# A router's logits on Trainium2: gate weights as the streamed operand, tokens as the stationary one

## The chip, the cores and the metric

The kernel runs on one core of a Trainium2 chip. The core has five engines that run side by side and wait for each other through semaphores: TensorE (PE; its weight loads are listed apart, as PEld), VectorE (DVE), ScalarE (ACT), GpSimd (POOL) and SyncE (SP), which issues most DMAs. Times are device microseconds (us) of one execution; the number that counts is the median of the runs.

## The reference, cut to what matters

Attention with a memory term over 4 batches, 8 heads and 576 positions gives x, 2304 tokens of 512 features. A mixture of 8 experts follows. Its router computes logits, takes the exponential, and normalises rows and columns eight times:

```
def _moe_ref(x, w_gate, w1, w2):
    N, D = x.shape                      # 2304, 512
    E = w_gate.shape[1]                 # 8
    logits = x @ w_gate
    logits = logits - logits.max()
    P = np.exp(logits)
    for _ in range(8):
        P /= P.sum(1, keepdims=True) + 1e-09
        P /= P.sum(0, keepdims=True) + 1e-09
        P *= N / E
    out = np.zeros((N, D), dtype=np.float32)
    for e in range(E):
        h = np.maximum(x @ w1[e], 0.0)
        ye = h @ w2[e]
        out += P[:, e:e + 1] * ye
```

## The kernel before, in words

Attention goes through 16 pairs of heads, one after another, in steps that overlap; the order of all instructions in it is written by hand: each step has a due time (pair number plus the number in the table WHEN), the steps are sorted by it, and every engine executes its own in that order. Each pair leaves 128 features of 576 tokens in two tiles, xh (rounded to a short mantissa) and xl (what the rounding dropped); `xh`, `xl` hold [128 features, 4 blocks of features, 2304 tokens].

The router's logits are made in five chunks of 512 tokens (the last has 256), `CHUNKS`. Three of them (0, 1, 2) stand in the hand-written order of attention, 0.33 of a pair after pairs 8, 12 and 16; two (3, 4) are tasks that are called between the parts of the first expert's product, outside the hand-written order.

`setup_router` (L173) puts the gate's weights into `wgp`, [128 features, 4 blocks, 128 columns]: columns 0 to 7 hold the rounded weights, 8 to 15 what the rounding dropped, and the other 112 are zeroed by a memset. `logits_a` (L707) uses one block of wgp, 128 by 128, as the stationary operand and streams 512 tokens of xh or xl past it: 8 matmuls for a chunk. The result has gate columns on partitions, so ScalarE copies 16 rows of it to `ls`. `logits_b` (L728) turns ls with small TensorE transposes, one for 128 tokens, into a second PSUM tile with tokens on partitions, and VectorE adds the two halves of 8 columns into `P`, [128 tokens, 18 blocks, 8 experts].

PSUM tiles of this kind come from a ring of six banks (`ps_s`, also called `ps_t`): each new tile takes the next bank, and waits until its last reader is done.

Other lines that are spoken of: L299, VectorE's subtractions that make ql and kl from the transposed q and k; L408, the scores; L540, transposes of the fifth block of exponentials; L648, the product with v; L678, GpSimd's subtraction that makes xl; L836 and L857, the first expert's two products.

Of the kernel before, what the change touches and what calls it, by code (L numbers as in the profile page):

```python
# [8 lines left out]
F32 = mybir.dt.float32  # L9
# [8 lines left out]
def kernel(  # L18
# [13 lines left out]
    nc = tc.nc  # L32
    B, H, S, D = q.shape
    NT, DM = out.shape
    E, _, F = w1.shape
    HP = H // 2
    KD = DM // 128
# [3 lines left out]
    CHUNKS = [(c, min(512, NT - c)) for c in range(0, NT, 512)]  # L41
# [8 lines left out]
    wst_p = ctx.enter_context(tc.tile_pool(name="wst", bufs=2))  # L50
    ps = ctx.enter_context(tc.tile_pool(name="ps", bufs=1, space=PSUM))

    xh = static.tile([128, KD, NT], F32R, name="xh")
    xl = static.tile([128, KD, NT], F32R, name="xl")
# [18 lines left out]
    ident = const.tile([128, 128], F32, name="ident")  # L73
    ones = const.tile([128, 128], F32, name="ones")
    wgp = const.tile([128, KD, 128], F32R, name="wgp")
# [21 lines left out]
    ps_t = ps_s  # L97
# [3 lines left out]
    def wst(w=512):  # L101
        wturn[0] += 1
        return wst_p.tile([128, w], F32, tag=f"wst{wturn[0] % 2}", name="wst", bufs=1)

    def f32(ap):
        return ap.bitcast(F32)
# [64 lines left out]
        nc.vector.tensor_copy(out=ogb, in_=g2[:, 1].unsqueeze(3).to_broadcast([128, HP, 2, 64]))  # L171

    def setup_router():  # L173
        nc.vector.memset(f32(wgp), 0.0)
        wgr = wst()
        wgv = wgr[:, 0:KD * E].rearrange("p (k e) -> p k e", e=E)
        nc.sync.dma_start(out=wgv, in_=wg.rearrange("(k p) e -> p k e", p=128))
        nc.vector.tensor_copy(out=wgp[:, :, 0:E], in_=wgv)
        nc.vector.tensor_tensor(
            out=wgp[:, :, E:2 * E], in0=wgv, in1=f32(wgp[:, :, 0:E]), op=ALU.subtract  # L180
        )
# [20 lines left out]
    }  # L202
    LATER = {
# [13 lines left out]
    def attention():  # L217
        with ExitStack() as actx:
# [66 lines left out]
            def steps(p):  # L285
# [398 lines left out]
            seq = [  # L684
                (p + WHEN[name] + LATER.get((p, name), 0.0), f)
                for p in range(NPAIR) for name, f in steps(p)
            ]
            for j in range(4):
                seq += [(0.5 + 0.5 * j + WHEN["w" + a], f) for a, f in zip("dhl", w_task(j))]
            for c, parts in enumerate(early_parts()):  # L690
                for i, t0, (a, d) in ((0, 8.33, "gA"), (1, 8.75, "gD")):
                    fs = (logits_a, logits_b)[i](c)
                    seq += [(4 * c + t0 + dt, f) for dt, f in zip((0.0, WHEN[a + d]), fs)]
                for j, fs in enumerate(parts):
                    t0 = 4 * c + 5 + j // 2 + (0.33, 0.75)[j % 2]
                    kinds = ("", "rA", "rD") if j < 2 else ("", "yD", "yS")
                    seq += [(t0 + WHEN.get(a, 0.0), f) for a, f in zip(kinds, fs)]
            seq += [(WHEN["sl"], load_gates), (WHEN["sg"], setup_gates)]
            seq.append((1.0, setup_router))
            seq.sort(key=lambda x: x[0])  # L700
            with tc.manual_schedule():
# [4 lines left out]
    lsd = {}  # L706

    def logits_a(c):
        c0, n = CHUNKS[c]

        def mm():
            lsd[c] = lp = ps_t()
            for a, x in enumerate((xh, xl)):
                for kt in range(KD):
                    nc.tensor.matmul(
                        out=lp[:, 0:n], lhsT=wgp[:, kt], rhs=x[:, kt, c0:c0 + n],
                        start=(a == 0 and kt == 0), stop=(a == 1 and kt == KD - 1),
                    )

        def take():  # L720
            lp = lsd[c]
            lsd[c] = ls = wst_p.tile([128, 512], F32, tag="ls", name="ls", bufs=1)[0:2 * E]
            nc.scalar.copy(out=ls[:, 0:n], in_=lp[0:2 * E, 0:n])

        return [mm, take]

    def logits_b(c):
        c0, n = CHUNKS[c]  # L728
        nt = n // 128

        def tr():
            ls = lsd[c]
            lsd[c] = lt = ps_t()
            for j in range(nt):
                nc.tensor.transpose(
                    lt[:, 16 * j:16 * j + 16], ls[:, 128 * j:128 * j + 128],
                    ident[0:2 * E, 0:2 * E],
                )

        def take():  # L740
            lv = lsd.pop(c)[:, 0:16 * nt].rearrange("p (t e) -> p t e", e=2 * E)
            pv_ = P[:, c0 // 128:c0 // 128 + nt]
            nc.vector.tensor_copy(out=pv_, in_=lv[:, :, 0:E])
            nc.vector.tensor_tensor(out=pv_, in0=lv[:, :, E:2 * E], in1=pv_, op=ALU.add)

        return [tr, take]

    def router_tasks():
        def both(f, c):
            for g in f(c):  # L750
                g()

        tasks = [lambda c=c, f=f: both(f, c) for c in (3, 4) for f in (logits_a, logits_b)]

        def max_a():
            nc.vector.reduce_max(mx[:, 0:1], P.rearrange("p t e -> p (t e)"), axis=AX.X)

        bank = {}

        def max_t():  # L760
            bank[0] = mt = ps.tile([128, 512], F32, tag="x", name="mt", bufs=1)
            nc.tensor.transpose(mt[:, 0:128], mx[:, 0:1].to_broadcast([128, 128]), ident)

        def max_b():
            mt = bank.pop(0)
            nc.vector.reduce_max(mx[:, 1:2], mt[:, 0:128], axis=AX.X)
            nc.vector.tensor_scalar_mul(mx[:, 1:2], mx[:, 1:2], -1.0)
            nc.scalar.activation(out=P, in_=P, func=AF.Exp, bias=mx[:, 1:2])

        def rows():  # L770
            nc.vector.reduce_sum(rs, P, axis=AX.X)
            nc.vector.tensor_scalar_add(rs, rs, 1e-9)
            nc.vector.reciprocal(out=rs, in_=rs)
            nc.vector.tensor_tensor(
                out=Pt, in0=P, in1=rs.unsqueeze(2).to_broadcast([128, NTILE, E]), op=ALU.mult
            )

        def colmat():
            bank[0] = cp = ps.tile([128, 512], F32, tag="x", name="cp", bufs=1)
            nc.tensor.matmul(  # L780
                out=cp[:, 0:NTILE * E], lhsT=ones, rhs=Pt.rearrange("p t e -> p (t e)"),
                start=True, stop=True,
            )

        def colsum():
            cp = bank.pop(0)
            nc.vector.reduce_sum(
                cs, cp[:, 0:NTILE * E].rearrange("p (t e) -> p e t", e=E), axis=AX.X
            )
            nc.vector.tensor_scalar_add(cs, cs, 1e-9)  # L790
            nc.vector.reciprocal(out=cs, in_=cs)
            nc.vector.scalar_tensor_tensor(
                out=P, in0=Pt, scalar=float(NT) / E,
                in1=cs.unsqueeze(1).to_broadcast([128, NTILE, E]), op0=ALU.mult, op1=ALU.mult,
            )

        tasks += [max_a, max_t, max_b]
        for _ in range(8):
            tasks += [lambda: None, rows, lambda: None, colmat, colsum][1:]

        def turn_p():
            bank[0] = mt = ps.tile([128, 512], F32, tag="x", name="mt", bufs=1)
            pf = wst()
            nc.vector.tensor_copy(
                out=pf[:, 0:144].rearrange("p (e t) -> p e t", e=E), in_=P.rearrange("p t e -> p e t")
            )
            nc.tensor.transpose(mt[0:126, 0:128], pf[:, 0:126], ident)
            nc.tensor.transpose(mt[0:18, 128:256], pf[:, 126:144], ident)

        def keep_p():  # L810
            mt, w = bank.pop(0), wst()
            rows_ = pd.rearrange("e (t c) -> (e t) c", c=128)
            nc.scalar.copy(out=w[0:126, 0:128], in_=mt[0:126, 0:128])
            nc.scalar.copy(out=w[0:18, 128:256], in_=mt[0:18, 128:256])
            nc.sync.dma_start(out=rows_[0:126], in_=w[0:126, 0:128])
            nc.sync.dma_start(out=rows_[126:144], in_=w[0:18, 128:256])

        return tasks + [turn_p, keep_p]
# [65 lines left out]
    def early_parts():  # L884
        def ps_f():
            return ps.tile([128, 512], F32, tag="f", name="f", bufs=1)

        return [first_parts(c, ps_f) for c in range(NEARLY)]
# [5 lines left out]
    def experts():  # L894
# [12 lines left out]
        ]  # L907
        acc = mg.tile([128, 2 * HT // 128, DM], F32, name="acc")
        tasks = router_tasks()
        tasks.reverse()  # L910

# [1050 lines left out]

    setup()
    attention()
    front.close()
    experts()
# [30 lines left out]
```

## Time and profile before

| what | us |
|---|---|
| runs shown | 1694.51, 1690.19, 1694.09 |
| median of them | 1694.09 |
| span of the profiled execution, first to last instruction | 1689.9 |
| TensorE busy in it | 1667.1 |
| VectorE, ScalarE, GpSimd busy | 1339.3, 692.2, 983.1 |
| attention, and the three early chunks of logits | 0 to about 244 |
| the two late chunks of logits | 247.7 to 257 |

The profile is of one execution; its own time is given only as the span. A row of the timeline has the start, the length, the engine, the line, the operation, the tiles (written<-read), stationary shape and streamed shape, and how many like it were merged; in square brackets stands how long the engine idled before it, and what ended that. A row of the chain has a start, a length and a line: it follows the work that ended last, back through what released each piece. A matmul's record is longer than the time until the next one may start, so its pace is read from starts.

### The profile page before, as it was taken

To read this page: it belongs to the slowest core of one execution; us is meant where nothing else is said; L and a number is where in the kernel's file an instruction comes from. 1 tells how busy PE (TensorE), PEld (TensorE's weight loads), DVE (VectorE), ACT (ScalarE), POOL (GpSimd) and SP (SyncE) were. 2 spreads that over 40 slices of the span, in tenths; PEclk is the share of its full clock that TensorE was granted. 3 is DMA by queue.
4 is the path that set the end of the run, shared out by engine and by line. 5 is a ranking of instruction groups with operands and counts; after the bars stand their busy time and mean duration, and the time that the engine had idled before them with its cause. 6 is when DMAs were issued, how large, how long until landed. Compare 5 with 4: busy or idle time off the path is not lost.

```text
span 1689.9 us, 29765 instructions
## 1 busy us (share of the span) xinstructions
PE 1667.1 (99%) x9779; PEld 1551.9 (92%) x9779; DVE 1339.3 (79%) x2805; ACT 692.2 (41%) x1724; POOL 983.1 (58%) x1036
## 2 busy tenths in 40 slices
PE   7999999999999999999999999999999999999998
PEld 6778778898998898889999999999999999999997
DVE  8877746867777777768898888989887878787887
ACT  7877752343433333334333333333243333333331
POOL 5755643578777877765556455455445544644561
PEclk9999999999999999999999999999999999999999
DMA  5443325478888888768787778677386767576663
GB/s 135 109 110 91 101 87 175 149 248 253 260 282 261 256 283 266 239 214 301 256 282 249 257 237 290 240 260 261 115 284 214 244 209 242 186 258 209 221 212 119
DMA packets 298145, 366.02 MB, mean 217 GB/s; under 512 B 80887, under 2 KB 176391, under 8 KB 297991
## 3 DMA queue, kind: packets, MB, share of 16 engines
q1 hardware_dynamic: 296215, 363.03, 66.8%
q8 instruction: 79, 1.29, 0.3%
q10 hardware_dynamic: 1776, 1.09, 0.2%
q14 instruction: 75, 0.61, 0.1%
HBM read 257.45 MB, written 106.58 MB: 215 GB/s over the span
## 4 chain that ended last, share of the span: by engine, by line
PE 91%; DVE 4%; DMA 2%; issue 1%; ACT 1%; POOL 0%; SPq 0%; DVEq 0%; ACTq 0%; POOLq 0%
PE s L1692 19%; PE s L1569 18%; PE s L857 14%; PE s L1111 10%; PE f L1569 6%; PE sx L1692 3%; PE f L1111 3%; PE x L648 2%; PE s L408 2%; PE f L1692 2%; PE s L1849 2%; PE s L489 1%; PE f L857 1%; PE f L836 1%; DVE temps L1548 1%; PE s L313 1%
## 5 line engine op out<-in xcount | busy, mean ns | idle before, releaser
L1548 DVE TENSOR_TENSOR temps<-s,temps 128x384 f32<-128x384 f32 x270 | 146.6, 553 | 91.6 <-PE s L1569 38.5
L1043 POOL TENSOR_TENSOR w1l<-raw,w1h 128x512 fp32r<-128x512 f32 x85 | 116.4, 1381 | 111.7 <-ACT w1h L1042 89.1
L1185 DVE SCALAR_TENSOR_TENSOR acc<-s,P,acc 128x512 f32<-128x512 f32 x168 | 123.1, 745 | 41.6 <-PE s L857 41.6
L857 PE MATMUL s<-w2h,hhh 128*128 128x512 f32 x372 | 146.0, 392 | 0.6 <-DVE acc L1185 0.6
L857 PE MATMUL s<-w2h,hhl 128*128 128x512 f32 x372 | 145.4, 391 | 0.0
L857 PE MATMUL s<-w2l,hhh 128*128 128x512 f32 x372 | 145.4, 391 | 0.0
L1548 DVE TENSOR_TENSOR m<-s,m 128x384 f32<-128x384 f32 x230 | 117.3, 550 | 7.5 <-PE s L1692 6.8
L1548 POOL TENSOR_TENSOR xl<-temps,xh 128x384 fp32r<-128x384 f32 x46 | 57.2, 1243 | 100.5 <-ACT xh L1590 100.5
L1590 ACT CAST xh<-temps 128x384 fp32r<-128x384 f32 x126 | 62.5, 513 | 118.1 <-DVE temps L1597 77.3
L1142 DVE TENSOR_TENSOR temps<-s,temps 128x384 f32<-128x384 f32 x132 | 71.4, 554 | 49.5 <-PE s L1111 39.4
L1569 PE MATMUL s<-xh,w1h 128*128 128x384 f32 x388 | 108.8, 335 | 0.0
L1597 DVE SCALAR_TENSOR_TENSOR temps<-temps,pb 128x384 f32<-128x384 f32 x180 | 105.5, 593 | 1.3
L1569 PE MATMUL s<-th,w1l 128*128 128x384 f32 x364 | 104.5, 334 | 0.0
L1569 PE MATMUL s<-th,w1h 128*128 128x384 f32 x356 | 102.3, 335 | 0.3 <-DVE temps L1548 0.3
L1076 POOL TENSOR_TENSOR w2l<-raw,w2h 128x512 fp32r<-128x512 f32 x62 | 97.5, 1591 | 2.8 <-ACT w2h L1075 2.8
L1095 ACT ACTIVATE hhh<-temps 128x384 fp32r<-128x384 f32 x100 | 52.5, 525 | 83.8 <-DVE temps L1142 82.8
L857 PEld LDWEIGHTS s<-w2h,hhh 128*128 128x128 f32 x372 | 69.9, 188 | 16.2 <-DVE acc L1185 2.6
L857 PEld LDWEIGHTS s<-w2h,hhl 128*128 128x128 f32 x372 | 69.8, 188 | 14.7
L857 PEld LDWEIGHTS s<-w2l,hhh 128*128 128x128 f32 x372 | 69.8, 188 | 13.7
L1096 DVE SCALAR_TENSOR_TENSOR hhl<-temps,hhh 128x384 fp32r<-128x384 f32 x100 | 81.3, 813 | 0.0
L1590 ACT CAST hb<-temps 128x384 fp32r<-128x384 f32 x90 | 46.1, 512 | 80.6 <-DVE temps L1597 79.9
L1548 POOL TENSOR_TENSOR temps<-temps,f 128x384 f32<-128x384 f32 x28 | 35.2, 1258 | 71.1 <-DVE hb L1548 40.8
(420 smaller groups left out, 5639.7 us busy)
## 6 DMA issues: line engine op xcount, KB each, us to landing
w1h<-cache SPq DMA_DIRECT2D x245, 256.0 KB
w1l<-cache SPq DMA_DIRECT2D x239, 256.0 KB
raw<-in_moe_w_dram SPq DMA_DIRECT2D x158, 256.0 KB
cache<-w1h SPq DMA_DIRECT2D x27, 896.0 KB
cache<-w1l SPq DMA_DIRECT2D x27, 896.0 KB
w2h<-cache SPq DMA_DIRECT2D x60, 256.0 KB
rawb<-in_moe_w_dram SPq DMA_DIRECT2D x32, 256.0 KB
cache<-w2h SPq DMA_DIRECT2D x31, 256.0 KB
```

What stands on the lines that cost most here:

```text
L857: nc.tensor.matmul(out=pt, lhsT=h_[:, f, cols], rhs=w[:, f], start=(n == 0), stop=(n == 5))
L1043: tt(out=wl[:, i:i + 2], in0=src, in1=f32(wh[:, i:i + 2]), op=ALU.subtract)
L1076: nc.gpsimd.tensor_tensor(out=wl[:, j], in0=raws[j], in1=f32(wh[:, j]), op=ALU.subtract)
L1096: late.append(lambda: nc.vector.scalar_tensor_tensor(out=hl[:, f, c], in0=src, scalar=0.0, in1=f32(hh[:, f, c]), op0=ALU.max, op1=ALU.subt ...
L1111: nc.tensor.matmul(out=pt[:, 0:HT], lhsT=w[:, wi, k], rhs=x[:, k], start=(n == 0), stop=(n == total - 1),)
L1142: nc.vector.tensor_tensor(out=o, in0=x, in1=y, op=ALU.add)
L1185: nc.vector.scalar_tensor_tensor(out=acc[:, j], in0=pt, scalar=P[:, t_, e:e + 1], in1=acc[:, j], op0=ALU.mult, op1=ALU.add,)
L1548: return lambda: eng.tensor_tensor(out=now_(o), in0=now_(x), in1=now_(y), op=op)
L1569: pe.matmul(out=bank[:, 0:HT], lhsT=w[:, a, k], rhs=x[b][:, k], start=bool(first and n == 0), stop=bool(last and n == 5),)
L1590: at(t, lambda: ac.copy(out=hop[j][n][0], in_=src), f"{n}H{j}")
L1597: at(t, lambda: dv.scalar_tensor_tensor(out=dst, in0=src, scalar=0.0, in1=pb[int(n[2]) - 1], op0=ALU.max, op1=ALU.mult), f"{n}F{j}")
L1692: pe.matmul(out=bank[n, a][:, 0:HT], lhsT=w[p][:, 128 * a:128 * a + 128], rhs=x[r], start=(j == js[0] and i == 0 and (n, a) not in held), ...
```

## The change

The operands of the logits change places. For each block of 128 tokens, xh and xl, 128 features by 128 tokens, are the stationary operand, and the 16 columns of wgp are streamed; four blocks of features times two (xh, xl) are eight matmuls for a block, 32 for a chunk of 512 tokens. The result has tokens on partitions at once. So ScalarE's copy to ls, the small transposes and the second PSUM tile are gone, as is the memset of the 112 columns, which nothing reads. `logits_b` is gone; its VectorE part, two instructions, is the second step of `logits_a` and takes its due time from "gD" after the matmuls, 0.42 of a pair earlier than before. For chunks 3 and 4 an empty task takes the place of logits_b.

```
     def setup_router():
-        nc.vector.memset(f32(wgp), 0.0)
...
             for c, parts in enumerate(early_parts()):
-                for i, t0, (a, d) in ((0, 8.33, "gA"), (1, 8.75, "gD")):
-                    fs = (logits_a, logits_b)[i](c)
-                    seq += [(4 * c + t0 + dt, f) for dt, f in zip((0.0, WHEN[a + d]), fs)]
+                seq += [(4 * c + 8.33 + dt, f) for dt, f in zip((0.0, WHEN["gD"]), logits_a(c))]
...
             lsd[c] = lp = ps_t()
-            for a, x in enumerate((xh, xl)):
+            for j in range(n // 128):
+                t = slice(c0 + 128 * j, c0 + 128 * j + 128)
                 for kt in range(KD):
-                    nc.tensor.matmul(
-                        out=lp[:, 0:n], lhsT=wgp[:, kt], rhs=x[:, kt, c0:c0 + n],
-                        start=(a == 0 and kt == 0), stop=(a == 1 and kt == KD - 1),
-                    )
+                    for a, x in enumerate((xh, xl)):
+                        nc.tensor.matmul(
+                            out=lp[:, 2 * E * j:2 * E * j + 2 * E], lhsT=x[:, kt, t],
+                            rhs=wgp[:, kt, 0:2 * E], start=(kt == 0 and a == 0),
+                            stop=(kt == KD - 1 and a == 1),
+                        )
 
         def take():
-            lp = lsd[c]
-            lsd[c] = ls = wst_p.tile([128, 512], F32, tag="ls", name="ls", bufs=1)[0:2 * E]
-            nc.scalar.copy(out=ls[:, 0:n], in_=lp[0:2 * E, 0:n])
-
-        return [mm, take]
-
-    def logits_b(c):
-        c0, n = CHUNKS[c]
-        nt = n // 128
-
-        def tr():
-            ls = lsd[c]
-            lsd[c] = lt = ps_t()
-            for j in range(nt):
-                nc.tensor.transpose(
-                    lt[:, 16 * j:16 * j + 16], ls[:, 128 * j:128 * j + 128],
-                    ident[0:2 * E, 0:2 * E],
-                )
-
-        def take():
-            lv = lsd.pop(c)[:, 0:16 * nt].rearrange("p (t e) -> p t e", e=2 * E)
+            nt = n // 128
+            lv = lsd.pop(c)[:, 0:2 * E * nt].rearrange("p (t e) -> p t e", e=2 * E)
             pv_ = P[:, c0 // 128:c0 // 128 + nt]
             nc.vector.tensor_copy(out=pv_, in_=lv[:, :, 0:E])
             nc.vector.tensor_tensor(out=pv_, in0=lv[:, :, E:2 * E], in1=pv_, op=ALU.add)
 
-        return [tr, take]
+        return [mm, take]
...
-        tasks = [lambda c=c, f=f: both(f, c) for c in (3, 4) for f in (logits_a, logits_b)]
+        tasks = [f for c in (3, 4) for f in (lambda c=c: both(logits_a, c), lambda: None)]
```

On TensorE, chunk 0 in the order of before, between the transposes of q and k for one pair and the product with v of the pair before it (x is the PSUM tile of that product, ls the copied logits):

```order
L330 MATMUL s<-ident,kraw_123 128x128
L331 MATMUL s<-ident,qraw_121 128x128
L715 MATMUL s<-xh,wgp 128x512 x4
L715 MATMUL s<-xl,wgp 128x512 x4
L648 MATMUL x<-eB,vs 64x320 x6
...
L489 MATMUL s<-ident,e 128x128 x11
L588 MATMUL s<-ident,qn_134 128x128
L735 MATMUL s<-ident,ls 128x16 x4
L540 MATMUL s<-ident,e_133 128x128 x4
```

The same place in the changed kernel, where the two rows of L714 alternate until there are 32 of them:

```order
L329 MATMUL s<-ident,kraw_123 128x128
L330 MATMUL s<-ident,qraw_121 128x128
L714 MATMUL s<-wgp,xh 128x16
L714 MATMUL s<-wgp,xl 128x16
...
L647 MATMUL x<-eB,vs 64x320 x6
...
L488 MATMUL s<-ident,e 128x128 x11
L587 MATMUL s<-ident,qn_134 128x128
L539 MATMUL s<-ident,e_133 128x128 x4
```

Eight long matmuls became 32 short ones at the same place, and the transposes of ls are gone; the rest stands as it did.

On VectorE, the same chunk before (P receives the logits; rr, ql, kl, rt and qp belong to the attention pairs):

```order
L559 TENSOR_TENSOR rr<-rm,rr 128x9
L299 TENSOR_TENSOR ql<-s,qh 128x512
L299 TENSOR_TENSOR kl<-s,kh 128x512
...
L480 COPY e_131<-s 128x128
...
L480 COPY eB<-s 128x3x128
L743 COPY P<-s 128x32
L744 TENSOR_TENSOR P<-s,P 128x32
L372 TENSOR_REDUCE rm<-tmp 128x8
```

And in the changed kernel:

```order
L558 TENSOR_TENSOR rr<-rm,rr 128x9
L724 COPY P<-s 128x32
L725 TENSOR_TENSOR P<-s,P 128x32
L298 TENSOR_TENSOR ql<-s,qh 128x512
L298 TENSOR_TENSOR kl<-s,kh 128x512
...
L479 COPY e_131<-s 128x128
...
L479 COPY eB<-s 128x3x128
L371 TENSOR_REDUCE rm<-tmp 128x8
```

The two instructions on P moved ahead of the four subtractions of ql and kl; chunk 1 moves in the same way. GpSimd and SyncE keep their instructions and their order; ScalarE loses the five copies to ls and nothing else.

## Rows read from the trace of the kernel before

**Rows 1.** The page: engines' busy time, and the chain's shares by engine.

```profile
PE 1667.1 (99%) x9779; PEld 1551.9 (92%) x9779; DVE 1339.3 (79%) x2805; ACT 692.2 (41%) x1724; POOL 983.1 (58%) x1036
...
PE 91%; DVE 4%; DMA 2%; issue 1%; ACT 1%; POOL 0%; SPq 0%; DVEq 0%; ACTq 0%; POOLq 0%
```

**Rows 2.** The chain of waits, 112 to 140 us: start, length, line, instructions.

```profile
116.75 0.44 PE s L540 x4
...
124.18 1.87 PE s L715 x8
...
130.32 0.35 PE s L735 x4
130.67 0.59 PE s L540 x4
...
132.02 2.07 PE s L408 x24
```

**Rows 3.** The chain of waits, 238 to 335 us: chunks 2, 3 and 4.

```profile
239.38 2.04 PE s L715 x8
...
252.57 0.35 PE s L735 x4
252.92 1.36 PE s L857 x5
254.28 0.24 PE s L715 x2
...
254.74 0.71 PE s L715 x6
...
256.84 0.22 PE s L735 x2
257.07 2.98 PE s L857 x12
```

**Rows 4.** The timeline of all engines, 238 to 275 us: start, length, instruction, [idle<-releaser].

```profile
247.18 0.19 PEld L836 LDWEIGHTS s<-xl,w1h 128*128 128x128 f32 x1 [0.56 <-POOL xl L678]
```

**Rows 5.** Weight loads by line and form, 123.9 to 131 us: count | busy, mean ns.

```profile
L715 PEld LDWEIGHTS s<-xl,wgp 128*128 128x128 f32 x4 | 0.8, 188 | 0.2
...
L735 PEld LDWEIGHTS s<-ident,ls 16*128 16x128 f32 x4 | 0.3, 137 | 0.2 <-PE s L489 0.2
```

**Rows 6.** The timeline of the weight loads, 130 to 132 us.

```profile
130.25 0.32 PEld L735 LDWEIGHTS s<-ident,ls 16*128 16x128 f32 x4 [0.17 <-PE s L489]
```

**Rows 7.** The timeline of TensorE, 260 to 292 us: first and last of 23 like matmuls.

```profile
260.12 0.28 PE L836 MATMUL s<-xl,w1h 128*128 128x256 f32 x1
...
262.63 0.28 PE L836 MATMUL s<-xh,w1l 128*128 128x256 f32 x1
```

**Rows 8.** The timeline of VectorE, 125.6 to 131.6 us.

```profile
126.11 0.69 DVE L299 TENSOR_TENSOR ql<-s,qh 128x512 fp32r<-128x512 f32 x1
126.72 1.02 DVE L299 TENSOR_TENSOR kl<-s,kh 128x512 fp32r<-128x512 f32 x3
129.92 0.29 DVE L480 COPY e<-s 128x128 f32<-128x128 f32 x1 [2.18 <-PE s L489]
...
131.43 0.19 DVE L744 TENSOR_TENSOR P<-s,P 128x32 f32<-128x32 f32 x1
```

**Rows 9.** The timeline of all engines, 22.6 to 24.6 us.

```profile
22.75 1.58 POOL L391 TENSOR_TENSOR vs<-vraw,ogb 128x640 f32<-128x640 f32 x1
...
23.09 0.48 DVE L174 MEMSET wgp<- 128x512 f32 x1 [0.17 <-issue]
...
23.61 0.76 DVE L178 CAST wgp<-wst 128x32 fp32r<-128x32 f32 x1
```

**Rows 10.** Busy time by stretch: us, busy of PE, PEld, DVE, ACT, POOL, granted clock, DMA.

```profile
15.90:19.30 3.40, 0.23 (x2) 0.23 (x3) 3.33 (x8) 3.04 (x12) 1.72 (x2) 1.00 0.72 185
19.30:22.70 3.40, 3.40 (x18) 3.40 (x17) 2.62 (x9) 1.13 (x3) 3.17 (x5) 0.50 0.18 28
...
323.20:326.60 3.40, 2.02 (x10) 1.46 (x9) 3.30 (x8) 0.00 (x0) 1.64 (x2) 1.00 0.98 281
```

2 rows, old and new, of the table WHEN are left out of this document.

## Prediction

> **What bounds the kernel now.** I read the page first: TensorE is busy for 99% of the span and makes up 91% of the chain of work that ended last [rows 1]. A busy share of matmuls says little here, because their records overlap; the chain says more, since each piece in it starts when the piece above it lets go. So I then read the chain in the two stretches where the router's logits stand. In the middle of attention (chunk 0 at 124 us; chunk 1 at 184.6 us shows the same pieces) every piece from 111.8 to 140 us, 44 of them, is TensorE, and the logits (L715) and the small transposes (L735) are two of them [rows 2]. After attention (chunks 2, 3 and 4) the chain is TensorE again [rows 3], with one excursion: the last pair's output goes through ScalarE and GpSimd to xl, and a weight load of L836 waits 0.56 us for that [rows 4]. So what these lines gain or lose on TensorE moves the end one for one, except where that wait swallows it. The copy on ScalarE and the two additions on VectorE are in no piece of it.
>
> **What leaves.** One 512-token chunk of logits costs 1.87 us for 8 matmuls, 0.234 each [rows 2]; chunks 0, 1 and 3 have this same row, three in all, and chunk 4 (256 tokens) costs 0.24 + 0.71 = 0.95 [rows 3]. The transposes cost 0.35, and the piece behind them is longer than it would be alone: 0.59 for four L540 transposes against 0.44 in a pair without logits, so 0.35 + 0.15 = 0.50 for chunks 0 and 1 [rows 2]. Chunk 3 gives 0.35 plus 1.36 - 5 x 0.234 = 0.19, together 0.54; chunk 4 gives 0.22 plus 2.98 - 12 x 0.234 = 0.17, together 0.39 [rows 3]. Chunk 2's transposes give nothing: they stand between the last attention matmul and the wait for xl, so that TensorE would only wait longer [rows 4]. Its logits, in contrast, stand ahead of the matmuls whose output feeds xl, so their time counts in full; of its 2.04 us [rows 3] I take 1.87 away, the rest being waits that stay.
>
> **What comes.** 18 blocks of 128 tokens, 8 matmuls each: 144 matmuls with a full 128x128 weight load and only 16 streamed columns. No row shows this shape, so the time from one to the next is bounded. From below: the removed transposes also stream 16 columns behind a load of 128 columns, and four loads took 0.32 us, of which the last alone is 0.137, so (0.32 - 0.137) / 3 = 0.061 from one to the next [rows 5, 6]. But a load of xh or xl is another kind: 0.188 against 0.137 for that one, 0.051 longer, which gives 0.061 + 0.051 = 0.112 [rows 5]. From above: nothing overlaps and each matmul costs its load's record, 0.188. Between them stands the same load behind a longer stream: 256 columns and a weight load of that type take (262.63 - 260.12) / 22 = 0.114 from one to the next, 22 steps in a row [rows 7]. At 2.4 GHz the 256 columns alone stream for 0.107, so this row does not say whether load or stream sets the pace, but fewer columns cannot make it slower while loads run ahead. I take 0.113, between the two estimates, since both are of this very load. A 512-token chunk then costs 32 x 0.113 = 3.62, chunk 4 costs 16 x 0.113 = 1.81.
>
> **The sum.** Chunks 0 and 1: 3.62 - 1.87 - 0.50 = +1.25 each. Chunk 2: 3.62 - 1.87 = +1.75. Chunk 3: 3.62 - 1.87 - 0.54 = +1.21. Chunk 4: 1.81 - 0.95 - 0.39 = +0.47. Together +5.9 us.
>
> **What costs or gives nothing.** The ScalarE copies (five) stood on an engine with no piece in these stretches; their removal gives nothing. VectorE's two instructions on P move up, ahead of the four subtractions of ql and kl, and so those now wait until the logits are done, near 127.8 (their piece ends at 124.18 + 1.87 = 126.05 now, and 1.75 later then), instead of starting at 126.11. They run until 127.74 in the trace, 1.63 us, and VectorE then sits idle for 2.18 us [rows 8]; behind the wait and P's 0.39 (131.23 to 131.62 in the trace) they end near 129.9, and their reader, the scores at 132.02 [rows 2], itself moves to about 133.3. That cover of some 3 us holds; if it were gone, each of chunks 0 and 1 would cost up to 2 us more. One PSUM bank per chunk is no longer taken, so all banks behind it move by one in the ring of six; no piece of the chain in these stretches is a wait for a bank. The memset of wgp, 0.48 us, stands on the chain early. But the cast behind it ends at 24.37, just behind GpSimd's 1.58 us that began at 22.75 and ends at 24.33, and takes 0.76 for 32 columns; I read that as waiting for GpSimd, so that removing the memset only lengthens the cast [rows 9]. Bounds: 0 to -0.48; I take 0. DMA queues and GpSimd issue the same instructions in the same order.
>
> **Against the profiled time.** The span is 1689.9 us, next to the fastest run shown (1690.19), so this execution would become 1695.8. The median of the runs is 1694.09; the sum moves it to **1700.0 us**, 0.35% slower. About 0.3% is what a measurement of this kernel can tell from no change, 5.1 us here, so the forecast is just outside it.
>
> **Rivals.**
> *The clock falls.* The granted clock was at half (1.2 GHz) from 19.3 to 22.7 us, and in the 3.4 us before that TensorE was busy for only 0.23 us, while a stretch with 2.02 of 3.40 us busy kept the full level (2.4 GHz) [rows 10]. The new blocks stream 16 columns per 0.113 us for 3.6 us on end; if the chip takes that for idleness, 3.4 us of what follows runs at half, which costs 1.7. Two of the four long blocks hit give 1700.0 + 3.4 = 1703.4, all four 1706.8. For it: so little streaming on end is nowhere else in the trace. Against it: the engine is loading weights all the time. The Trainium skill ("TensorE: Matmul & The Clock Gate", HAM oscillation — how this bites in real kernels) says that too thin a loop puts the engine back to the slow level again and again; the trace shows that only after true idleness.
> *Loads are as fast as the transposes'.* Then each new matmul costs 0.061 instead of 0.113, 144 x 0.052 = 7.5 less: 1692.5, not slower. It decides from 0.113 - 5.9 / 144 = 0.072 downward, where the sum is zero. Against it: 0.188 for the loads of xh and xl [rows 5]. The Trainium skill ("TensorE: Matmul & The Clock Gate", Weight-path perf modes — Fast Weight Load (FWL) and DoubleRow) has a fast load for 128 weights of any type but FP32, which would be a rule for this rival if it covered the rounded type; the load rows speak against that.
> *Attention swallows its share.* If VectorE's wait or a bank set the pace in pairs 8 to 13, the 2 x 1.25 us of chunks 0 and 1 would fall into other waits: 1697.5. Against it: the unbroken chain of TensorE pieces there [rows 2].
> *Loads and matmuls in turn.* 0.188 each gives 144 x 0.075 = 10.8 more: 1710.8. Against it: the steps of 0.114 with loads of 0.188 [rows 5, 7].
>
> **How the numbers follow.** Forecast 0.55, clock 0.17, fast loads 0.13, swallowed 0.11, in turn 0.04. With 0.109 to 0.120 for a step the forecast's own range is 1699.4 to 1701.0, and the runs before lie 4 us apart, so I give it 1696 to 1702. The range 1693 to 1706 takes in the swallowed case and most of the clock's, and leaves out the fast loads and the serial case. Slower: most of the forecast (0.40 of its 0.55), the clock and the serial case, 0.61. Within the bound: the rest of the forecast, the swallowed case and most of the fast loads, 0.35. Faster: 0.04, fast loads together with the memset's 0.48.
>
> **What would show it.** In the trace after: the chain should hold 32 steps of logits at about 3.6 us per chunk with no transposes behind; weight loads of 0.188 back to back; VectorE waiting for TensorE ahead of the P copy, and no wait at the scores; the wait for xl longer than before by about 0.5; the granted clock at 1.00 through 124 to 260 us; the cast of wgp still ending with GpSimd's instruction. It is wrong if the steps lie near 0.06 or near 0.19, if the clock shows a second dip, or if the logits grow by 1.75 a chunk and the pairs behind them do not start later.

## The result: 17 us slower, three times the forecast loss

| | median us | runs | lowest to highest |
|---|---|---|---|
| before | 1692.38 | 4 | 1690.19 to 1694.51 |
| changed | 1709.55 | 4 | 1707.52 to 1710.39 |

The ratio is 1.0098, with a 95% interval of 1.0086 to 1.0110: about 17 us slower, where the forecast said 5.9, or 1700.0, and the range ended at 1706. The profiled execution has a span of 1705.7 us against 1689.9, 15.8 more.

The page of the changed kernel, TensorE's busy time and the chain by engine, answers to [rows 1]:

```profile
PE 1682.6 (99%) x9865; PEld 1565.4 (92%) x9865; DVE 1342.4 (79%) x2804; ACT 690.1 (40%) x1719; POOL 983.8 (58%) x1036
...
PE 90%; DVE 5%; DMA 2%; issue 1%; POOL 1%; ACT 0%; SPq 0%; DVEq 0%; POOLq 0%; ACTq 0%
```

Nothing in it points to a new bound: TensorE grew by 15.5 us and still is the chain. Where it grew stands in the chain itself. First chunk 0, which answers to [rows 2]; the first two lines are the same pieces behind the product with v one pair earlier, for comparison:

```profile
110.86 2.21 PE x L647 x20
113.06 0.43 PE x L652 x4
...
123.96 3.47 PE s L714 x32
127.43 3.27 PE x L647 x20
130.71 0.85 PE x L652 x4
```

The logits take 3.47 us, which the prediction had at 3.62. But the 20 matmuls behind them, which nobody touched, take 3.27 us in place of 2.21, and the 4 of L652 behind those 0.85 in place of 0.43. Something slows TensorE down after the new block. Chunk 1, the same view:

```profile
187.11 4.03 PE s L714 x32
191.14 4.25 PE x L647 x20
```

Here the logits themselves are longer (4.03) and the product with v behind them takes nearly twice its time. After attention, answering to [rows 3]:

```profile
246.25 3.67 PE s L714 x32
249.92 2.21 PE x L647 x20
...
256.40 4.95 PE s L714 x32
261.35 4.58 PE s L817 x12
```

Chunk 2 (246.25) does no harm to what follows; chunk 3 (256.40) takes 4.95 us, and the 12 matmuls behind it 4.58, against 2.80 for the same piece before:

```profile
247.91 1.87 PE s L715 x8
249.78 2.80 PE s L836 x12
...
260.05 0.11 PE mt L762
```

The view that explains all of it is busy time by stretch with the granted clock, which answers to [rows 10]. The columns are the stretch, its length, busy time of PE, PEld, DVE, ACT and POOL, the granted clock, the share of DMA and GB/s. The kernel before:

```profile
120.00:260.00 140.00, 139.87 (x1104) 109.67 (x1102) 89.56 (x327) 95.92 (x299) 72.61 (x96) 1.00 0.37 104
```

And the changed kernel, its stretches at 0.50 cut where the granted clock changes:

```profile
125.00:128.41 3.41, 3.41 (x30) 2.97 (x31) 1.32 (x7) 1.61 (x6) 2.25 (x4) 1.00 0.38 87
128.41:131.82 3.41, 3.41 (x23) 2.04 (x20) 1.00 (x4) 0.48 (x1) 1.96 (x3) 0.50 0.00 0
...
189.85:196.68 6.83, 6.83 (x37) 4.37 (x37) 1.91 (x6) 0.48 (x1) 3.63 (x4) 0.50 0.02 4
...
258.12:264.94 6.82, 6.82 (x25) 6.05 (x25) 0.38 (x2) 1.24 (x3) 2.65 (x3) 0.50 0.93 308
```

Three stretches stand at 0.50, which is 1.2 in place of 2.4 GHz: 3.41, 6.83 and 6.82 us, 17.06 together, where the kernel before has none between 23 us and its last 2 us. Half of that, up to 8.5 us, is lost if all of TensorE's work in them takes twice its time. The first line is what the engine did just ahead of the first fall: it was busy for all of the 3.41 us. In [rows 10] the clock fell behind 0.23 us of work in 3.40; here it fell behind a stretch without any idleness, 2.43 us of which belong to L714.

To set the sum of the prediction against the trace without the scatter of the rest, I use one interval that all kernels but e2_spread, whose order differs, share: from the start of chunk 0's first matmul of logits to the start of the transpose that follows chunk 4 (written to mt). The two rows, from the timelines of TensorE, of the kernel before, of the changed one and of the first experiment below:

```profile
123.94 1.18 PE L715 MATMUL s<-xh,wgp 128*128 128x512 f32 x4
...
259.89 0.27 PE L762 MATMUL mt<-ident,mx 128*128 128x128 f32 x1
```

```profile
123.72 0.26 PE L714 MATMUL s<-wgp,xh 128*128 128x16 f32 x1
...
273.30 0.27 PE L743 MATMUL mt<-ident,mx 128*128 128x128 f32 x1
```

```profile
124.39 0.31 PE L715 MATMUL s<-wgp,xh 128*128 128x128 f32 x1
...
266.22 0.27 PE L744 MATMUL mt<-ident,mx 128*128 128x128 f32 x1
```

Before it is 135.95 us, after 149.58: +13.63. The steps (5.9) and half of the half-clock stretches (8.5) make 14.4, so the two terms account for it to within 0.8. The first experiment, e1_wide, has 141.83, +5.88, and is told next.

### The profile page after: what moved, and what is told of

Same layout as the page of the kernel before. It is cut to its first block, busy times and chain, and to the rows that moved or that the text cites. A ratio compares the mean times of both kernels' runs of the same rounds, so it can differ in the third digit from the quotient of the medians.

```text
span 1705.7 us, 29928 instructions
## 1 busy us (share of the span) xinstructions
PE 1682.6 (99%) x9865; PEld 1565.4 (92%) x9865; DVE 1342.4 (79%) x2804; ACT 690.1 (40%) x1719; POOL 983.8 (58%) x1036
## 4 chain that ended last, share of the span: by engine, by line
PE 90%; DVE 5%; DMA 2%; issue 1%; POOL 1%; ACT 0%; SPq 0%; DVEq 0%; POOLq 0%; ACTq 0%
PE s L1673 19%; PE s L1550 17%; PE s L838 14%; PE s L1092 10%; PE f L1550 6%; PE sx L1673 3%; PE f L1092 3%; PE x L647 3%; PE s L407 2%; PE f L1673 2%; PE s L1830 2%; PE s L488 1%; DVE temps L1529 1%; PE s L714 1%; PE f L838 1%; PE f L817 1%
```

## The experiments

The theory after the first look: the steps cost what was forecast, and the rest is TensorE's clock, which falls because the new blocks stream so little for so long. Rival A: it falls because of the dense weight loads, whatever is streamed. Rival B: the clock is a side show and the loss comes from later work.

### e1_wide: the same loads, more streamed columns

```
+        nc.vector.memset(f32(wgp), 0.0)
...
-                            out=lp[:, 2 * E * j:2 * E * j + 2 * E], lhsT=x[:, kt, t],
-                            rhs=wgp[:, kt, 0:2 * E], start=(kt == 0 and a == 0),
+                            out=lp[:, 128 * j:128 * j + 128], lhsT=x[:, kt, t],
+                            rhs=wgp[:, kt], start=(kt == 0 and a == 0),
...
-            lv = lsd.pop(c)[:, 0:2 * E * nt].rearrange("p (t e) -> p t e", e=2 * E)
+            lv = lsd.pop(c)[:, 0:n].rearrange("p (t e) -> p t e", e=128)
```

> The changed kernel, but each of the 144 matmuls streams all 128 columns of wgp (112 of them zero, so the memset is back) in place of 16; the weight loads, their number and their place stay. Theory (thin streaming lowers the clock, and that costs what goes beyond the +5.9 us of the steps): a step stays near 0.113 us, since the load sets it; granted clock 1.00 through 120 to 270 us; about +6 us against the kernel before, logits pieces of about 3.5 us per chunk, no matmul at half speed behind them. Rival A (back-to-back weight loads lower the clock, whatever is streamed): the stretches at 0.50 stay near 128, 190 and 258 us, +13 to +17 us. Rival B (the clock matters little, the rest of the loss comes from later work that moved): +13 to +17 us with the clock at 1.00.

Measured: 1697.76 us, ratio 1.0027 (1.0018 to 1.0037), 4.8 us more than the 1692.93 of the kernel before beside it. Its chain at chunk 0, and busy time by stretch (columns as above):

```profile
124.63 3.52 PE s L715 x32
128.15 2.21 PE x L648 x20
```

```profile
124.40:128.10 3.70, 3.70 (x37) 3.63 (x34) 1.36 (x5) 2.88 (x10) 1.27 (x3) 1.00 0.39 86
...
100.00:280.00 180.00, 179.56 (x1446) 147.65 (x1445) 111.17 (x394) 112.41 (x350) 90.46 (x118) 1.00 0.38 105
```

Eight times as many columns take the same 3.5 us, and what stands behind them runs at its old 2.21. The granted clock is 1.00 from 100 to 280 us. The loads are as many and as dense as in the changed kernel (3.63 us of PEld in 3.70), so rival A is out. So is rival B as the main cause: the later work is the same, and the loss is 4.8 us in place of 17. Streaming 112 columns of zeros makes the changed kernel 10 to 12 us faster, by the medians. The interval from chunk 0 to mt is 5.88 longer than before, against the 5.9 of the prediction.

The profile is of one execution, but the mean granted clock is listed for each. It is 0.998 to 1.000 in the ten of e1_wide, 0.997 to 1.000 in the 36 of the kernel before that ran beside the experiments, and 0.992 to 0.994 in eight of the nine of the changed kernel (with the repeats below). The ninth lists 0.944 at 1710.39 us; that would be some 190 us at half clock, which its time doesn't show, and stays unexplained.

### e2_spread: the same matmuls, cut up

The blocks of a chunk get due times of their own (the bank of the first expert's product, free at that time, holds the early chunks), and the late ones tasks of their own:

```
-                seq += [(4 * c + 8.33 + dt, f) for dt, f in zip((0.0, WHEN["gD"]), logits_a(c))]
+                due = (0.33, 0.345, 0.87, 1.1, 1.2) if c < 2 else (0.1, 0.33, 0.7, 0.72, 0.73)
+                seq += [(4 * c + 8 + dt, f) for dt, f in zip(due, logits_a(c))]
...
+        l3, l4 = logits_a(3), logits_a(4)
+        tasks = [
+            l3[0], l3[1], lambda: None, l3[2], lambda: None, lambda: [f() for f in l3[3:]],
+            l4[0], lambda: [f() for f in l4[1:]],
+        ]
...
-                if c == NEARLY:
-                    tick()
+                tick()
```

Here tick() calls the next task, now behind every part of the first expert's product in chunks 3 and 4.

> The changed kernel with the same 144 matmuls of 16 columns, but each chunk cut into its blocks of 8 matmuls (0.9 us), with 1.4 to 3 us of other matmuls between two blocks in most places (two pairs of blocks stay together, 1.8 us); the tile for the early chunks is the bank of the first expert's product, which is free then. Theory (a long thin stretch lowers the clock): no stretch at 0.50 between 100 and 270 us, about +5.5 us against the kernel before (the 144 steps cost the same, and blocks behind the last pair's product fill the wait for xl, worth 0.5). Rival A (weight loads as such): 8 loads of this kind in a row stand elsewhere in the kernel without harm, so also no dips: this run does not tell it from the theory. Rival B (loss comes from elsewhere): still +13 to +17 us.

Measured: 1698.09 us, ratio 1.0030 (1.0019 to 1.0042), +5.2. By stretch:

```profile
100.00:280.00 180.00, 180.00 (x1450) 148.54 (x1448) 112.05 (x395) 113.38 (x352) 91.17 (x117) 1.00 0.38 105
```

The same 144 matmuls of 16 columns, with other work between the blocks, leave the clock at 1.00. So it isn't the thin matmuls as such but their standing together that costs, and the 5 us of steps stay in either kernel. By the order of the work alone the changed kernel gets back 10 to 12 us; it still doesn't reach the kernel before.

### e3_early and e4_late: one half of the change each

In e3_early chunks 0, 1 and 2 have the new form, in e4_late chunks 3 and 4; the others keep logits_a and logits_b as they were before (old_a, old_b), and both keep the memset. The diff against the changed kernel, e3_early:

```
-        tasks = [f for c in (3, 4) for f in (lambda c=c: both(logits_a, c), lambda: None)]
+        tasks = [lambda c=c, f=f: both(f, c) for c in (3, 4) for f in (old_a, old_b)]
```

and e4_late:

```
-                seq += [(4 * c + 8.33 + dt, f) for dt, f in zip((0.0, WHEN["gD"]), logits_a(c))]
+                for i, t0, (a, d) in ((0, 8.33, "gA"), (1, 8.75, "gD")):
+                    fs = (old_a, old_b)[i](c)
+                    seq += [(4 * c + t0 + dt, f) for dt, f in zip((0.0, WHEN[a + d]), fs)]
```

> The new form for chunks 0, 1 and 2 alone; chunks 3 and 4 in the form of the kernel before (with its copies and small transposes, and the memset back). Theory: +4.25 us of steps, and the stretches at 0.50 behind chunk 0 and at chunk 1 stay (3.4 + 6.8 us long, 5.1 us lost): about +9 us against the kernel before, clock 1.00 from 200 us to the end of attention and on. Rival B: about the same share of the loss without dips. If chunk 2 has a dip here, the total is about +11.

> The new form for chunks 3 and 4 alone; chunks 0, 1 and 2 in the form of the kernel before. Theory: +1.7 us of steps and one stretch at 0.50 near 250 us of 3.4 to 6.8 us (1.7 to 3.4 us lost): +3.4 to +5.1 us against the kernel before, clock 1.00 from 24 us to there. If it and the kernel with the early chunks alone add up to the whole loss of the change (about 15 in the span), nothing outside the five chunks is needed to explain it; a sum well short of that speaks for rival B.

Measured: e3_early 1698.28 us, ratio 1.0037 (1.0024 to 1.0050), +5.4 where about +9 was expected; e4_late 1695.74 us, 1.0017 (1.0008 to 1.0026), +2.8 where +3.4 to +5.1 was expected. By stretch, e3_early:

```profile
128.12:131.53 3.41, 3.41 (x14) 1.66 (x16) 1.90 (x6) 0.00 (x0) 3.14 (x4) 0.50 0.00 0
...
247.58:251.00 3.42, 3.42 (x14) 1.64 (x16) 0.38 (x2) 0.00 (x0) 0.06 (x1) 0.50 0.00 0
```

and e4_late:

```profile
253.45:256.86 3.41, 3.41 (x10) 2.62 (x9) 0.00 (x0) 0.03 (x1) 0.69 (x1) 0.50 1.03 380
```

In e3_early the half-clock stretches stand behind chunks 0 and 2, not at 0 and 1 as I had expected, each 3.41 us; in the interval to mt it is 7.52 behind, against 4.25 + 3.41 = 7.66 worked out. In e4_late there is one of 3.41; +3.23 against 1.68 + 1.71 = 3.39. Each kernel by itself follows the rule "steps plus half of the half-clock stretches". But the two do not add up to the change (+8.2 in the medians against +17): the expectation for e4_late called that a case for rival B. In these two profiles the half-clock stretches sum to 10.24 us, in the changed kernel's to 17.06, which is 3.4 us of the difference; the next runs ask whether that is chance.

### a_again and a_look: the changed kernel twice more

No edit.

> The changed kernel once more, unchanged, next to the kernel before on one chip: the early-only and late-only kernels add up to about +8 to +9 us, the change itself to +17, and this asks where the rest is. Theory (thin stretches lower the clock for 3.4 or 6.8 us, depending on where a chunk's block falls against the chip's own rhythm, which no kernel sets): stretches at 0.50 again between 100 and 275 us, two to four of them, but not of the same lengths and places as in the first profile; by 290 us the kernel is behind by 5.9 us plus half their sum, within 1 us; the median +12 to +17 us. Rival B (something else in the later part costs the rest): by 290 us no more than +9, and several us lost between 290 us and the end in every execution.

> The changed kernel a third time, for its profile alone. Theory: as above, 5.9 us plus half of the sum of the stretches at 0.50 by 290 us, with places and lengths of the stretches of its own. Rival B: the delay by 290 us does not follow the stretches.

Measured: a_again 1708.23 us, ratio 1.0092 (1.0077 to 1.0107), +15.4; a_look, one run, 1707.84. By stretch, a_again and then a_look, only the stretches at 0.50 between 100 and 275 us:

```profile
128.76:132.17 3.41, 3.41 (x15) 1.77 (x16) 1.91 (x6) 0.00 (x0) 3.19 (x4) 0.50 0.01 1
...
248.22:251.64 3.42, 3.42 (x15) 1.65 (x16) 0.38 (x2) 0.00 (x0) 0.43 (x1) 0.50 0.00 0
...
258.46:265.29 6.83, 6.83 (x23) 5.93 (x24) 0.38 (x2) 1.26 (x3) 2.65 (x3) 0.50 0.92 303
```

```profile
129.36:132.77 3.41, 3.41 (x25) 2.20 (x22) 0.84 (x3) 0.48 (x1) 1.79 (x3) 0.50 0.00 0
...
190.80:197.62 6.82, 6.82 (x38) 4.36 (x37) 1.91 (x6) 0.48 (x1) 3.50 (x4) 0.50 0.01 2
...
259.06:265.89 6.83, 6.83 (x25) 5.96 (x25) 0.38 (x2) 1.25 (x3) 2.65 (x3) 0.50 0.89 297
```

The same program doesn't always have its half-clock stretches in the same places: behind chunks 0 and 3 in all three profiles, at chunk 1 in two, behind chunk 2 in one. a_look repeats the first profile in places and lengths, which was not expected; a_again differs. All kernels together, by the interval from chunk 0's first logits to mt, against 135.95 before:

| kernel | longer by, us | steps forecast | half-clock stretches, us | steps + half of them |
|---|---|---|---|---|
| e1_wide | 5.88 | 5.9 | 0 | 5.9 |
| e4_late | 3.23 | 1.68 | 3.41 | 3.4 |
| e3_early | 7.52 | 4.25 | 6.83 | 7.7 |
| a_again | 12.06 | 5.9 | 13.66 | 12.7 |
| changed, first profile | 13.63 | 5.9 | 17.06 | 14.4 |
| a_look | 13.62 | 5.9 | 17.06 | 14.4 |

The order is kept throughout, and no row is off by more than 0.8. e3_early and e4_late add up to 10.75; with half of the half-clock time that a_again and a_look have beyond theirs (13.66 and 17.06 against 10.24) that makes 12.5 and 14.2, against 12.06 and 13.62. So up to mt, at 273 us, the theory stands, and the two halves of the change add up.

Beyond mt something is open. From that transpose to the end of the span the kernel before takes 1430.0 us, e1_wide, e3_early, e4_late and e6_fill (below) 1428.4 to 1430.9, and the three profiles of the changed kernel 1431.9 to 1432.4: about 2 us more than before, although e1_wide does the same work there. That much of rival B is left. It comes in steps of less than 1 us in the experts' products, and no run here shows the cause. a_again has one more stretch at 0.50 there, 3.41 us at 770.5, behind 3.41 us in which TensorE was busy for 1.42. But e1_wide has one like it at 763.0 and loses nothing behind mt, so that is not the cause either.

### e6_fill: the old form, put behind the last product

The kernel before with chunk 2's logits moved behind the last pair's product with v, where TensorE waits for xl [rows 4]:

```
-                for i, t0, (a, d) in ((0, 8.33, "gA"), (1, 8.75, "gD")):
+                for i, t0, (a, d) in ((0, 8.33 + 0.35 * (c == 2), "gA"), (1, 8.75 + 0.2 * (c == 2), "gD")):
```

> The kernel before with one move: chunk 2's eight matmuls stand behind the last pair's product with v, in place of ahead of it, and its small transposes a little later, so that TensorE has 1.87 us of work while ScalarE and GpSimd make the last xl. Theory (whatever stands in front of the last product with v counts in full, whatever stands behind it first fills the wait for xl, 0.56 us there): the wait is gone and the first expert's products behind it start 0.5 us earlier than before; in the whole time -0.5 us, too little to be told from none. Rival (the wait only moves to another reader of xl or to a PSUM bank): no gain in the trace.

Measured: 1692.87 us, ratio 0.9997 (0.9988 to 1.0007). The chain:

```profile
243.69 2.07 PE s L715 x8
245.76 0.93 PE s L836 x4
246.69 0.35 PE s L735 x4
```

No wait for xl is left in it. But the interval to mt is shorter by 0.14 us only, not by 0.5: the small transposes, 0.35, which cost nothing while they stood in front of that wait, now are a piece of the chain. The wait's 0.56 less that 0.35 leaves 0.2. It is less than the runs can tell from none, as the ratio shows, and no version that beats both kernels came out of these runs.

## Why the prediction was wrong, step by step

**What the trace bore out.** The step of the logits: first and last of chunk 0's 32 matmuls start at 123.72 and 127.18, which makes 3.46 / 31 = 0.112 us, against 0.113 taken. Weight loads run back to back at 192 ns a record; these are chunk 0's loads of xl (columns as in [rows 5]):

```profile
L714 PEld LDWEIGHTS s<-wgp,xl 128*128 128x128 f32 x16 | 3.1, 192 | 0.0
```

The columns do not set the pace, since e1_wide's steps with 128 columns are 0.113; that the load does is the reading that is left, not a separate test.

The sum of +5.9 came out as +5.88 up to mt where the clock stayed up, and as +4.8 and +5.2 in the medians of e1_wide and e2_spread. That the 5.88 is so close is in part luck, as the chain of e1_wide shows:

```profile
133.62 2.07 PE s L408 x23
...
242.15 3.72 PE s L715 x32
...
252.35 3.52 PE s L715 x32
...
266.38 0.11 PE mt L744
```

From the logits of chunk 0 (124.63) to the scores it is 8.99 us against 7.84 before, +1.15 where 1.25 was forecast. Chunk 2's logits gain 3.72 - 2.04 = 1.68 where 1.75 was forecast. Chunks 3 and 4, up to mt, take 14.03 against 12.14, +1.89 where 1.68 was forecast. The errors cancel.

The memset: GpSimd's instruction and the cast of wgp now read, in the timeline of all engines (answering to [rows 9])

```profile
22.54 1.58 POOL L390 TENSOR_TENSOR vs<-vraw,ogb 128x640 f32<-128x640 f32 x1
...
22.64 1.51 DVE L177 CAST wgp<-wst 128x32 fp32r<-128x32 f32 x1
```

The cast takes 1.51 us in place of 0.76 and ends at 24.15, just behind GpSimd's 24.12, as it ended just behind it before: nothing gained, as taken. VectorE's move, answering to [rows 8], its timeline:

```profile
127.47 0.19 DVE L724 COPY P<-s 128x32 f32<-128x32 f32 x1 [1.61 <-PE s L714]
...
128.40 1.01 DVE L298 TENSOR_TENSOR kl<-s,kh 128x512 fp32r<-128x512 f32 x3
132.93 0.29 DVE L479 COPY e<-s 128x128 f32<-128x128 f32 x1 [3.52 <-PE s L488]
```

It waits for the logits (1.61) and then for TensorE again (3.52), so no reader of ql and kl was held up: kl is done at 129.41, and the scores start at 134.53 in the chain. And the wait for xl, answering to [rows 4], grew, but not by the 0.5 that was forecast:

```profile
254.72 0.19 PEld L817 LDWEIGHTS s<-xh,w1h 128*128 128x128 f32 x1 [0.19 <-POOL xh L674]
255.67 0.19 PEld L817 LDWEIGHTS s<-xl,w1h 128*128 128x128 f32 x1 [0.76 <-POOL xl L677]
```

It went from 0.56 to 0.76, and a wait of 0.19 for xh stands ahead of it. Together that is 0.39 more, in place of the 0.35 of the transposes that used to stand in this time. So chunk 2's transposes gave nothing, as taken.

**What failed.** It is the clock. The forecast held it at 1.00 through 124 to 260 us, so that in the sum it stood at nothing, and as the first rival it was wrong in both of its numbers.

Its chance was 0.17, on the argument that the engine loads weights all the time. The stretch 125.00 to 128.41, busy for 3.41 us out of 3.41 and followed by 0.50, shows that busyness of this kind did not hold the clock, and e1_wide shows that the loads did not bring it down.

Its price was 1.7 us for a block that is hit, half of 3.4. Of the nine half-clock stretches that the profiles of the changed kernel show between 100 and 275 us, five lasted 6.83 us, 3.4 lost each. In all five a good part of the block itself (1.0 to 3.2 us) ran in the half-clock stretch; in the four of 3.41 the block was over or within 0.4 us of its end when the clock fell. The prediction had two blocks of four at 1.7, 1703.4, and all four, 1706.8. Three blocks with 1.7 + 3.4 + 3.4 on top of the 5.9 make 14.4, and so 1708.5 from the median used then. From the 1692.38 of all four runs they make 1706.8; the 2.8 from there to the measured 1709.55 is about what stays open behind mt.

The Trainium skill ("TensorE: Matmul & The Clock Gate", HAM oscillation — how this bites in real kernels) tells of a thin loop whose waits for data bring the slow level back each time. The trace has the fall without such a wait, 0.50 behind 3.41 us of work in 3.41, and the measurement decides. I had read the one row at hand, a dip behind idleness, as evidence against the rival, though that row says only that idleness is enough, not that it is needed.

The range left this case out for the most part: it ended at 1706, as if no more than three of the short falls could come together (1700.0 + 3 x 1.7 = 1705.1).

## What to carry to other kernels

Swapping the operands to make the streamed side small trades columns for weight loads: here 8 matmuls of 0.234 became 32 of 0.112, since a step cost as much with 16 columns as with 128, and the copy and transposes that this saved were off the path or worth 0.5 a chunk. A long run of such matmuls can also lower TensorE's clock for work that has nothing to do with it, so look at the granted clock behind the block and not only at the block's own time. If the form is wanted for another reason, spread the blocks among wide matmuls, or stream padding that the load's time covers anyway: either took back 10 to 12 us here.

## What the runs showed that I had not expected

- More work was faster: 128 streamed columns in place of 16 took the same time a step (0.113 against 0.112 us) and made the kernel 10 to 12 us faster; up to mt the clock accounts for that.
- The half-clock stretches at the logits came as 3.41 or 6.83 us, and one program placed them differently in one of three executions, while the medians of its two sets of runs (1709.55 and 1708.23) lie 1.3 us apart.
- Two halves of a change need not add up in the whole time: +5.4 and +2.8 against +15.4 to +17.2. Up to mt they do, once the half-clock time of each execution is counted.
